# Off-diagonal blocks of the 64x64 inverses: both chunks of a pass at once, even heads from the left and odd heads from the right

## Chip, cores and metric

The kernel runs on one core of one Trainium2 chip. The metric is the device time of one execution in microseconds (us); the number given for the kernel before is the median of three runs. TensorE is called PE here (its weight loads PEld), VectorE DVE, ScalarE ACT, GpSimd POOL and SyncE SP, as in the profile.

## What is computed

Three layers follow each other: a delta-rule linear attention over 4 batches of 8 heads (768 tokens, head size 48), and two feed-forward layers on its 3072 tokens (384 to 2048 to 384).

```python
for t in range(S):                      # attention, per batch and head
    y[t]  = q[t] @ state
    v_old = k_n[t] @ state              # k_n is k divided by its norm
    state = state + beta[t] * outer(k_n[t], v[t] - v_old)
...
h = x @ w_in                            # layer 1
x = where(h > 0, h, exp(min(h, 0)) - 1) @ w_out
h = x @ w_in2                           # layer 2
out = (h * sigmoid(1.702 * h)) @ w_out2
```

All of it is float32. The kernel splits the operands of the feed-forward layers into a high and a low part and does three matmuls for one.

## The kernel before, in words

**Chunks and passes.** The attention is done in 12 chunks of 64 tokens, two to a pass, so there are 6 passes (0 to 5) of 128 tokens. In a chunk the recurrence becomes a triangular system per head, and its 64x64 inverse is needed. The 32 head-batch pairs ("heads" from here) of a chunk lie in 16 columns `u` by two halves of the partitions: partitions 0 to 63 hold one head and 64 to 127 another. A pass holds its inverses in the tile `z`, 128 x 32 x 64; chunk `2p` has `z[:, 0:16]`, chunk `2p + 1` has `z[:, 16:32]`.

**The inverse.** `inverse(p)` (line 199) builds the two 32x32 diagonal blocks of each 64x64 inverse on DVE, both chunks of the pass together; in passes 0 to 2 (`FINE`) it does 16x16 blocks, and `join16` (line 299) joins these by matmuls. The off-diagonal 32x32 block is then formed as minus (inverse of the second block) x (the block of the Gram matrix between them) x (inverse of the first). That takes three steps of `chunk(c)` (line 331), once for each chunk:

- `t2` (line 381): one DVE transpose of the chunk's diagonal blocks, 128 x 512.
- `m1` (line 385): 32 matmuls of 32x32x32 (line 392), each float32 matmul being two records in the trace. Every one reads the partitions 32 to 63 or 96 to 127 and writes 0 to 31 or 64 to 95 of one PSUM bank (`bank()`, tag `at`). ACT evacuates it with two copies of 32 x 512 (line 396) and copies the diagonal blocks beside themselves, 128 x 512 (line 398); POOL clears two pieces of 32 x 512 (line 400).
- `m2` (line 402): 32 matmuls of 32x32x32 (line 407), reading and writing partitions 0 to 31 and 64 to 95, into a bank of the same tag. ACT evacuates with two activations of 32 x 512 (line 412) into `z`.

The other steps of a chunk are `kq` (scores of keys and queries, line 362, masked by DVE in `mask`, line 377), `ks` (keys by state, line 423, subtracted from the values by DVE, line 428), `w` (the inverse times that, line 440, evacuated by ACT), `state` (line 459, added by DVE, line 462), `y` (line 474) and `out` (transposes, line 496). They use the tile `wide()` (line 118): two PSUM banks with one buffer, so that each step that takes `wide` waits until the one before has been evacuated. The tag `at` has one buffer of one bank. PSUM is full: two banks of tag `h`, three of `acc`, two of `wide`, one of `at`.

**The order of the work.** All of it is one list per engine, written in program order (`manual_schedule`). The backbone is 192 units: layer 1 has 96 (6 passes x 16 slices of the 2048 hidden channels), then layer 2. In unit `t`, `up` issues 12 matmuls of 128x128x512 (line 576) and `down` of unit `t - 2` another 12 (line 610; line 621 in layer 2). ACT and DVE turn `h` into `gh` and `gl` between (lines 585 to 601). The attention of pass p is set among the units of layer 1's pass p - 1 by tables in `schedule()` (line 685): a slot `s` means unit `s // 2`, in the middle (`mid`, between `up` and `down`) if even and at its end (`end`, after `down`) if odd. `fill` holds steps of the next inverse and of the weight split, which `spread()` places with the help of `taken`, the load that `VECTOR` (line 943) assigns to a step. Entries of one slot run in the order of the table.

For passes 3 to 5 the table of before (line 851) reads `(6, a, "t2"), (6, a, "m1"), (6, a, "kq"), (8, a, "m2"), (9, b, "t2"), (9, b, "m1"), (9, a, "ks"), (11, b, "m2"), (11, a, "w")`, with `a` and `b` the two chunks. Pass 1 (lines 831 to 835) and pass 2 (line 849) have tables of their own in which these steps lie farther apart. Pass 0 is written out by hand.

Of the kernel before, what the change touches and what calls it, by code (L numbers as in the profile page):

```python
# [9 lines left out]
F32 = mybir.dt.float32  # L10
# [3 lines left out]
AF = mybir.ActivationFunctionType  # L14
# [6 lines left out]
P = 128  # L21
NP = S // P
# [9 lines left out]
class Kernel:  # L32
# [94 lines left out]

    def place(self, c, name):

        if c in (0, 2):  # L130
            x, i = (self.spare[0], 0) if name == "t2" else (self.spare[1], 1024)
            return x[:, i:i + 512].rearrange("p (u t) -> p u t", u=16)
        return self.ap.tile([P, 16, 32], F32, name=name, tag=name)

# [192 lines left out]
        return turned, left, right  # L327

    def chunk(self, c):

# [352 lines left out]
    def schedule(self):  # L685
        nc = self.nc
# [6 lines left out]
        def at(where, u, *fns):  # L693
            where.setdefault(u, []).extend(fns)
# [15 lines left out]

        names = ("nv", "t2", "m1", "kq", "mask", "m2", "ks", "w", "state", "y", "out")
        ch = {c: dict(zip(names, self.later(lambda c=c: list(self.chunk(c).values()), len(names)))) for c in range(NC)}


        spare = self.spare = [self.mp.tile([P, NK * TB], F32, name=n, tag=n) for n in ("xh", "xl")]
# [113 lines left out]
        for slot, c, i in ((5, 2, 0), (5, 2, 1), (7, 2, 2), (8, 3, 0), (8, 3, 1), (10, 3, 2)):  # L829
            at(end if slot % 2 else mid, slot // 2, join[c][i])  # L830
        for slot, c, name in (
# [3 lines left out]
        ):  # L835
            u = slot // 2
            at(end if slot % 2 else mid, u, ch[c][name])
            taken[u] = taken.get(u, 0.0) + self.VECTOR.get(name, 0.0)
        at(end, 7, lambda: self.load_v(3))
# [5 lines left out]
        for p in range(2, NP):  # L845
            o = base[p - 1]
            a, b = 2 * p, 2 * p + 1
            first = (
                (6, a, "t2"), (6, a, "m1"), (8, a, "m2"), (10, a, "kq"), (11, a, "ks"), (12, b, "t2"), (12, b, "m1"), (13, a, "w"), (14, b, "m2"),
            ) if p in self.FINE else (  # L850
                (6, a, "t2"), (6, a, "m1"), (6, a, "kq"), (8, a, "m2"), (9, b, "t2"), (9, b, "m1"), (9, a, "ks"), (11, b, "m2"), (11, a, "w"),
            )
            late = 2 if p in self.FINE else 0
            for slot, c, name in first + (
                (13 + late, a, "state"), (15 + late, a, "y"), (15 + late, b, "nv"), (17 + late, b, "ks"), (19 + late, b, "w"),
                (21 + late, b, "state"), (23, a, "out") if not late else (22, a, "out"), (25, b, "kq"), (27, b, "y"), (29, b, "out"),
            ):
                u = o + slot // 2
                at(end if slot % 2 else mid, u, ch[c][name], *([ch[c]["mask"]] if name == "kq" else []))
                taken[u] = taken.get(u, 0.0) + self.VECTOR.get(name, 0.0)  # L860
            at(end, o - 2, lambda a=a: self.load_kt(a), lambda a=a: self.load_q(a), lambda a=a: self.load_v(a))
            at(end, o - 1, lambda a=a: self.load_kn(a), lambda b=b: self.load_kt(b), lambda b=b: self.load_q(b))
            at(end, o + 2, ch[a]["nv"])
            at(end, o + 5, lambda b=b: self.load_v(b))
            at(end, o + 7, lambda b=b: self.load_kn(b))
            taken[o] = taken.get(o, 0.0) - 0.48
            taken[o + 2] = taken.get(o + 2, 0.0) - 0.48
            taken[o + 1] = taken.get(o + 1, 0.0) + 0.4
        for p in range(2, NP):
            o = base[p - 1]  # L870
# [21 lines left out]
        for t in range(len(units) + self.LAG):  # L892
            if t == len(units):
                low()
            if t < len(units):
                kind, p, c0, n, m = units[t]
# [43 lines left out]
        return [0.1, 1.9, 0.2, 0.7] + [0.8] * (1 if p < 2 else 3) + [1.7, 1.2] + rows + [1.4, 1.9]  # L940


    VECTOR = {"kq": 0.15, "t2": 0.26, "m1": -0.44, "m2": -0.44, "ks": -0.1, "w": -0.44, "state": 0.15, "y": -0.74, "out": 0.17}
    LAG = 2
    N2 = 10
    FINE = 0, 1, 2
# [96 lines left out]
```

## Time and profile before

| what | value |
|---|---|
| device time, median of 3 runs | 1046.31 us (1043.93 to 1048.43) |
| profiled execution, span of the core | 1047.7 us |
| PE busy | 996.2 us, 95% |
| DVE busy | 591.2 us, 56% |
| ACT busy | 453.4 us, 43% |
| POOL busy | 49.5 us, 5% |
| mean granted TensorE clock | 0.974 |

The profile is of one execution, whose span runs from the first to the last instruction; of that execution the page gives the span alone, and it lies within the three runs, 1.4 us above their median. "Granted clock" is the share of full speed that TensorE was given: it has two levels, 1.00 (2.4 GHz) and 0.50 (1.2 GHz). A matmul's row gives when it was issued and how long it took from issue to its last result; since matmuls overlap in the array, the cost of a block of them is read from the start of its first to the start of the next block's first. Idle time stands in brackets with what ended it; "issue" means that the profile shows nothing that was waited for.

### The profile page before, as it was taken

The numbers are of one execution on the slowest core, as the hardware profiler recorded it, in microseconds if no ns is written. First come the engines' busy times: TensorE is split into PE (matmuls) and PEld (weight loads), VectorE is DVE, ScalarE is ACT, GpSimd is POOL, SyncE is SP. The second block draws the span as 40 slices with busy tenths as digits, with TensorE's granted clock in tenths as the row PEclk, the third lists the DMA queues.
The fourth block names the chain that finished last, engine by engine and source line by source line (L and its number), as shares of the span: only waits on it lengthen the run. The fifth ranks groups of instructions, "written<-read, shape, count | busy, mean of one in ns | idle before, by whom it ended". The sixth has DMA issues, their size and how long they took to land.

```text
span 1047.7 us, 26839 instructions
## 1 busy us (share of the span) xinstructions
PE 996.2 (95%) x12136; PEld 854.1 (82%) x12136; DVE 591.2 (56%) x1021; ACT 453.4 (43%) x749; POOL 49.5 (5%) x65
## 2 busy tenths in 40 slices
PE   2678898999999999999999999999999999999998
PEld 2666776877788888888888788999999999999997
DVE  5579568837786777668434676743333333333333
ACT  1254575544445445545544766533333333333322
POOL 2000000000001000000000010000100001000000
PEclk9677999999999999999999999999999999999999
DMA  5252341401220221211001741001010010010000
GB/s 178 114 174 97 114 153 53 132 34 61 63 91 20 72 77 53 71 39 65 18 17 61 281 201 61 1 1 61 1 53 9 1 61 1 23 38 1 31 1 31
DMA packets 20178, 68.40 MB, mean 65 GB/s; under 512 B 3168, under 2 KB 6240, under 8 KB 20064
## 3 DMA queue, kind: packets, MB, share of 16 engines
q1 hardware_dynamic: 20064, 66.69, 18.7%
q8 instruction: 95, 1.56, 0.6%
q14 instruction: 19, 0.16, 0.0%
HBM read 57.25 MB, written 9.44 MB: 64 GB/s over the span
## 4 chain that ended last, share of the span: by engine, by line
PE 92%; DVE 4%; issue 2%; DMA 1%; ACT 1%; SPq 0%; ACTq 0%; DVEq 0%
PE h L576 38%; PE acc L610 18%; PE acc L621 10%; PE accn L621 10%; PE ps_w L362 2%; PE ps_w L474 2%; PE ps_w L459 2%; PE ps_w L188 2%; PE ps_b L392 1%; PE ps_b L407 1%; PE ps_w L423 1%; DMA kg<-in_kT 1%; PE ps_w L440 1%; PE ps_w L496 1%; PE ps_b L323 1%
## 5 line engine op out<-in xcount | busy, mean ns | idle before, releaser
L576 PE MATMUL h<-xh,wt 128*128 128x512 f32 x1152 | 401.0, 402 | 6.4 <-DVE wt L555 5.0
L576 PEld LDWEIGHTS h<-xh,wt 128*128 128x128 f32 x1152 | 219.5, 191 | 53.2 <-DVE wt L555 6.3
L576 PE MATMUL h<-xl,wt 128*128 128x512 f32 x576 | 229.4, 398 | 0.0
L610 PE MATMUL acc<-gh,wt 128*128 128x512 f32 x576 | 197.0, 396 | 0.5 <-DVE xo L674 0.5
L598 ACT CAST gh<-t 128x512 fp32r<-128x512 f32 x192 | 119.2, 621 | 174.8 <-DVE t L589 118.7
L601 DVE TENSOR_TENSOR gl<-t,gh 128x512 fp32r<-128x512 f32 x192 | 138.7, 723 | 68.1 <-PE acc L621 30.9
L595 DVE TENSOR_TENSOR t<-t,h 128x512 f32<-128x512 f32 x96 | 66.0, 688 | 180.3 <-ACT t L592 180.2
L592 ACT ACTIVATE t<-h 128x512 f32<-128x512 f32 x96 | 57.4, 598 | 198.9 <-PE h L576 198.9
L610 PEld LDWEIGHTS acc<-gh,wt 128*128 128x128 f32 x576 | 108.9, 189 | 24.4 <-issue 0.9
L576 PEld LDWEIGHTS h<-xl,wt 128*128 128x128 f32 x576 | 109.8, 191 | 19.2 <-DVE xl L502 0.2
L610 PE MATMUL acc<-gl,wt 128*128 128x512 f32 x288 | 112.9, 392 | 0.0
L589 DVE SCALAR_TENSOR_TENSOR t<-t,h 128x512 f32<-128x512 f32 x96 | 65.6, 684 | 76.2 <-ACT t L586 75.7
L585 ACT ACTIVATE t<-h 128x512 f32<-128x512 f32 x96 | 57.4, 598 | 113.5 <-PE h L576 112.8
L621 PE MATMUL acc<-wt,gh 128*128 128x384 f32 x384 | 98.5, 337 | 0.0
L621 PE MATMUL accn<-wt,gh 128*128 128x384 f32 x384 | 98.1, 336 | 0.0
L621 PEld LDWEIGHTS accn<-wt,gh 128*128 128x128 f32 x384 | 71.0, 188 | 5.4
L621 PEld LDWEIGHTS acc<-wt,gh 128*128 128x128 f32 x384 | 70.3, 188 | 2.8
L621 PE MATMUL acc<-wt,gl 128*128 128x384 f32 x192 | 64.9, 338 | 0.0
L621 PE MATMUL accn<-wt,gl 128*128 128x384 f32 x192 | 64.8, 337 | 0.0
L610 PEld LDWEIGHTS acc<-gl,wt 128*128 128x128 f32 x288 | 54.4, 189 | 10.3
L586 ACT ACTIVATE t<-t 128x512 f32<-128x512 f32 x96 | 60.6, 632 | 3.0
L640 POOL TENSOR_TENSOR xl<-x1r,xh 128x512 fp32r<-128x512 f32 x18 | 24.4, 1355 | 413.9 <-ACT xh L639 321.8
(143 smaller groups left out, 968.7 us busy)
## 6 DMA issues: line engine op xcount, KB each, us to landing
raw<-in_w SPq DMA_DIRECT2D x32, 768.0 KB, 7.4
kt<-in_kT SPq DMA_DIRECT2D x12, 512.0 KB, 4.6
x<-in_qT SPq DMA_DIRECT2D x24, 256.0 KB, 4.2
kg<-in_kT SPq DMA_DIRECT2D x10, 512.0 KB, 4.7
vn<-in_vn SPq DMA_DIRECT2D x12, 384.0 KB, 4.3
kn<-in_kn SPq DMA_DIRECT2D x12, 384.0 KB, 3.6
x1d<-xo SPq DMA_DIRECT2D x12, 384.0 KB, 2.9
x1r<-x1d SPq DMA_DIRECT2D x6, 768.0 KB, 4.6
```

Of the source, the lines that this page charges most:

```text
L188: self.nc.tensor.matmul(o[q:q + 32], k[:, 32 * sub:32 * sub + 32], x, start=True, stop=True)
L576: nc.tensor.matmul(hps, wt[:, part, k * P:(k + 1) * P], src[:, k, c], start=(i == 0), stop=(i == 3 * NK - 1))
L585: nc.scalar.activation(out=t, in_=hps, func=AF.Relu, scale=-1.0)
L586: nc.scalar.activation(out=t, in_=t, func=AF.Exp, scale=-1.0)
L589: nc.vector.scalar_tensor_tensor(out=t, in0=t, scalar=-1.0, in1=hps, op0=ALU.add, op1=ALU.max)
L592: nc.scalar.activation(out=t, in_=hps, func=AF.Sigmoid, scale=1.702)
L595: nc.vector.tensor_tensor(out=t, in0=t, in1=hps, op=ALU.mult)
L598: nc.scalar.copy(gh, t)
L601: nc.vector.tensor_tensor(out=gl, in0=t, in1=gh.bitcast(F32), op=ALU.subtract)
L610: self.nc.tensor.matmul(acc[c], wt[:, part, DM + c * P:DM + (c + 1) * P], src, start=(m == 0 and i == 0), stop=(m == NM - 1 and i == 2),)
L621: self.nc.tensor.matmul(acc[w], src[:, c], wt[:, part, DM:2 * DM], start=(m == 0 and i == 0), stop=(m == NM - 1 and i == 2),)
L640: nc.gpsimd.tensor_tensor(out=xl, in0=raw, in1=xh.bitcast(F32), op=ALU.subtract)
```

## The change

In passes 1 to 5 the steps `t2`, `m1` and `m2` are no longer those of `chunk` but of a new method, `across(p)`, which does each once for both chunks of a pass: one transpose of 128 x 1024, 64 matmuls in `m1` and 64 in `m2`. Heads with even `u` are formed as before, from the left. For heads with odd `u` the product is taken in the other order: `m1` reads the partitions of the first block and writes those of the second, and `m2` reads there and writes the first's. So the matmuls of a step go through four different groups of 32 partitions instead of two. `m1` keeps one bank of tag `at` (the odd heads now fill the other partitions of the same bank) and is evacuated by one copy of 128 x 512; `m2` takes both banks of `wide`, evens in one and odds in the other, and is evacuated by two activations of 32 x 1024. The copy inside `z` is 128 x 1024, the two clears 32 x 1024. The transposed blocks lie in spare tiles in pass 1 and in the tile of tag `kg` in passes 2 to 5. Pass 0 keeps its steps. The tables are rewritten, and three values of `VECTOR`.

```diff
--- before.py
+++ after.py
@@ -127,10 +127,18 @@
 
     def place(self, c, name):
 
-        if c in (0, 2):
+        if c == 0:
             x, i = (self.spare[0], 0) if name == "t2" else (self.spare[1], 1024)
             return x[:, i:i + 512].rearrange("p (u t) -> p u t", u=16)
         return self.ap.tile([P, 16, 32], F32, name=name, tag=name)
+
+    def places(self, p):
+
+        if p == 1:
+            t, m = self.spare[0][:, 0:1024], self.spare[1][:, 1024:1536]
+            return t.rearrange("p (u t) -> p u t", u=32), m.rearrange("p (u t) -> p u t", u=16)
+        t = self.ap.tile([P, 16, 64], F32, name="kg", tag="kg").rearrange("p u (b t) -> p (u b) t", b=2)
+        return t, self.ap.tile([P, 16, 32], F32, name="m1", tag="m1")
 
 
 
@@ -327,6 +335,46 @@
         return turned, left, right
 
 
+
+    def across(self, p):
+
+        nc, pe, act = self.nc, self.nc.tensor, self.nc.scalar
+        s, own = self.pas[p], {}
+
+        def t2():
+            own["t2"], own["m1"] = self.places(p)
+            nc.vector.transpose(out=own["t2"], in_=s["z"][:, :, 0:32])
+
+        def m1():
+            z, t = s["z"], own["t2"]
+            ps = self.bank().rearrange("p (v t) -> p v t", v=16)
+            for u in range(32):
+                for o in (0, 64):
+                    near, far = slice(o, o + 32), slice(o + 32, o + 64)
+                    if u % 2:
+                        pe.matmul(ps[far, u // 2, :], z[near, u, 32:64], t[near, u, :], start=True, stop=True)
+                    else:
+                        pe.matmul(ps[near, u // 2, :], z[far, u, 32:64], z[far, u, 0:32], start=True, stop=True)
+            act.copy(own["m1"], ps)
+            act.copy(z[:, :, 32:64], z[:, :, 0:32])
+            for o in (0, 64):
+                nc.gpsimd.memset(z[o + 32:o + 64, :, 0:32], 0.0)
+
+        def m2():
+            z, t, m = s["z"], own["t2"], own["m1"]
+            ps = self.wide().rearrange("p b (v t) -> p b v t", v=16)
+            for u in range(32):
+                for o in (0, 64):
+                    near, far = slice(o, o + 32), slice(o + 32, o + 64)
+                    a, b = (m[far, u // 2, :], z[far, u, 32:64]) if u % 2 else (t[near, u, :], m[near, u // 2, :])
+                    pe.matmul(ps[near, u % 2, u // 2, :], a, b, start=True, stop=True)
+            for o in (0, 64):
+                near = slice(o, o + 32)
+                act.activation(
+                    out=z[near, :, 32:64].rearrange("p (v b) t -> p b v t", b=2), in_=ps[near], func=AF.Copy, scale=-1.0
+                )
+
+        return dict(t2=t2, m1=m1, m2=m2)
 
     def chunk(self, c):
 
@@ -710,6 +758,10 @@
 
         names = ("nv", "t2", "m1", "kq", "mask", "m2", "ks", "w", "state", "y", "out")
         ch = {c: dict(zip(names, self.later(lambda c=c: list(self.chunk(c).values()), len(names)))) for c in range(NC)}
+        for p in range(1, NP):
+            for name, f in zip(("t2", "m1", "m2"), self.later(lambda p=p: list(self.across(p).values()), 3)):
+                ch[2 * p][name] = f
+                del ch[2 * p + 1][name]
 
 
         spare = self.spare = [self.mp.tile([P, NK * TB], F32, name=n, tag=n) for n in ("xh", "xl")]
@@ -829,8 +881,8 @@
         for slot, c, i in ((5, 2, 0), (5, 2, 1), (7, 2, 2), (8, 3, 0), (8, 3, 1), (10, 3, 2)):
             at(end if slot % 2 else mid, slot // 2, join[c][i])
         for slot, c, name in (
-            (4, 2, "kq"), (4, 2, "mask"), (7, 2, "nv"), (9, 2, "t2"), (9, 2, "m1"), (10, 3, "kq"), (10, 3, "mask"),
-            (11, 2, "m2"), (12, 3, "t2"), (12, 3, "m1"), (13, 2, "ks"), (14, 3, "m2"), (15, 2, "w"), (17, 2, "state"), (17, 3, "nv"),
+            (4, 2, "kq"), (4, 2, "mask"), (7, 2, "nv"), (10, 2, "t2"), (10, 3, "kq"), (10, 3, "mask"),
+            (11, 2, "m1"), (13, 2, "m2"), (13, 2, "ks"), (15, 2, "w"), (17, 2, "state"), (17, 3, "nv"),
             (18, 2, "y"), (20, 3, "ks"), (22, 3, "w"), (24, 3, "state"), (25, 2, "out"), (26, 3, "y"), (28, 3, "out"),
         ):
             u = slot // 2
@@ -846,9 +898,9 @@
             o = base[p - 1]
             a, b = 2 * p, 2 * p + 1
             first = (
-                (6, a, "t2"), (6, a, "m1"), (8, a, "m2"), (10, a, "kq"), (11, a, "ks"), (12, b, "t2"), (12, b, "m1"), (13, a, "w"), (14, b, "m2"),
+                (9, a, "t2"), (10, a, "m1"), (10, a, "kq"), (12, a, "m2"), (12, a, "ks"), (14, a, "w"),
             ) if p in self.FINE else (
-                (6, a, "t2"), (6, a, "m1"), (6, a, "kq"), (8, a, "m2"), (9, b, "t2"), (9, b, "m1"), (9, a, "ks"), (11, b, "m2"), (11, a, "w"),
+                (6, a, "t2"), (6, a, "kq"), (7, a, "m1"), (9, a, "m2"), (9, a, "ks"), (11, a, "w"),
             )
             late = 2 if p in self.FINE else 0
             for slot, c, name in first + (
@@ -940,7 +992,7 @@
         return [0.1, 1.9, 0.2, 0.7] + [0.8] * (1 if p < 2 else 3) + [1.7, 1.2] + rows + [1.4, 1.9]
 
 
-    VECTOR = {"kq": 0.15, "t2": 0.26, "m1": -0.44, "m2": -0.44, "ks": -0.1, "w": -0.44, "state": 0.15, "y": -0.74, "out": 0.17}
+    VECTOR = {"kq": 0.15, "t2": 0.55, "m1": -0.5, "m2": -0.5, "ks": -0.1, "w": -0.44, "state": 0.15, "y": -0.74, "out": 0.17}
     LAG = 2
     N2 = 10
     FINE = 0, 1, 2
```

## Rows read from the trace of the kernel before

**Rows 1.** The page: span, TensorE's busy time, and the chain by engine.
```profile
span 1047.7 us, 26839 instructions
...
PE 996.2 (95%) x12136; PEld 854.1 (82%) x12136; DVE 591.2 (56%) x1021; ACT 453.4 (43%) x749; POOL 49.5 (5%) x65
...
PE 92%; DVE 4%; issue 2%; DMA 1%; ACT 1%; SPq 0%; ACTq 0%; DVEq 0%
```

**Rows 2.** Windows: busy us (count) of PE, PEld, DVE, ACT, POOL; granted clock; DMA.
```profile
160.00:200.00 40.00, 36.80 (x629) 29.49 (x628) 34.23 (x75) 21.46 (x34) 1.20 (x2) 0.96 0.35 111
320.00:360.00 40.00, 40.00 (x720) 32.88 (x719) 29.03 (x65) 18.00 (x30) 3.34 (x5) 1.00 0.19 58
230.00:1047.00 817.00, 812.54 (x7466) 702.28 (x7464) 436.94 (x734) 348.06 (x570) 35.47 (x35) 1.00 0.15 50
```

**Rows 3.** Timeline of PE, pass 5: start us, us, line, tiles, count.
```profile
506.14 0.39 PE L576 MATMUL h<-xl,wt 128*128 128x512 f32 x1
506.36 0.39 PE L576 MATMUL h<-xh,wt 128*128 128x512 f32 x1
506.68 1.20 PE L407 MATMUL ps_b<-m,t 32*32 32x32 f32 x64
507.81 0.50 PE L610 MATMUL acc<-gh,wt 128*128 128x512 f32 x1
508.15 0.40 PE L610 MATMUL acc<-gl,wt 128*128 128x512 f32 x1
...
511.21 1.15 PE L423 MATMUL ps_w<-su,kt 48*64 48x48 f32 x64
512.28 0.50 PE L576 MATMUL h<-xh,wt 128*128 128x512 f32 x1
```

**Rows 4.** Timeline of PE, pass 2: a block of `join16`, then a gap inside one.
```profile
209.98 1.26 PE L315 MATMUL ps_b<-kg,z 32*32 32x16 f32 x128
211.17 0.50 PE L610 MATMUL acc<-gh,wt 128*128 128x512 f32 x1
...
215.34 0.85 PE L323 MATMUL ps_b<-w 16*32 16x16 f32 x79 [1.31 <-issue]
```

**Rows 5.** Timeline of PE, pass 1: two more gaps.
```profile
126.38 0.45 PE L362 MATMUL ps_w<-x,kt 48*64 48x64 f32 x8 [0.86 <-issue]
...
135.83 1.15 PE L423 MATMUL ps_w<-su,kt 48*64 48x48 f32 x64
138.05 1.48 PE L188 MATMUL ps_w<-kg 48*32 48x64 f32 x128 [1.08 <-DVE r L428]
```

**Rows 6.** Groups of instructions from 114 to 600 us: busy us, mean ns.
```profile
L412 ACT ACTIVATE z<-ps_b 32x512 f32<-32x512 f32 x20 | 11.7, 583 | 0.7 <-PE ps_b L407 0.5
...
L428 DVE TENSOR_TENSOR r<-vn,ps_w 128x768 f32<-128x768 f32 x10 | 9.5, 954 | 15.2 <-PE ps_w L423 15.2
...
L194 ACT COPY z<-ps_w 128x1024 f32<-128x1024 f32 x7 | 7.1, 1013 | 4.9 <-PE ps_w L188 4.9
L383 DVE STREAM_TRANSPOSE t<-z 128x512 f32<-128x512 f32 x9 | 6.3, 705 | 0.0
```

**Rows 7.** Windows behind gaps of TensorE; granted clock behind POOL's column.
```profile
126.40:178.00 51.60, 48.25 (x911) 38.44 (x911) 40.54 (x65) 32.69 (x53) 2.62 (x4) 1.00 0.31 106
...
178.90:182.20 3.30, 3.27 (x11) 2.92 (x12) 1.14 (x3) 1.58 (x3) 0.00 (x0) 0.50 0.00 0
...
216.50:219.80 3.30, 3.30 (x9) 2.31 (x7) 2.85 (x5) 0.00 (x0) 0.00 (x0) 0.50 0.02 7
```

**Rows 8.** Chain of waits in order of time: start us, us, what.
```profile
216.18 3.84 PE h L576 x9
...
224.61 2.26 PE h L576 x9
```

**Rows 9.** Waits of PE: us in total, times, longest us.
```profile
PE ps_w L496 <- DVE su L462: 2.6, 1, 2.6
...
PE ps_w L423 <- DVE x L377: 0.4, 1, 0.4
```

## The prediction

> **What bounds the kernel now.** I read the page first. TensorE is busy for 996.2 of 1047.7 us, and 92% of the chain that ended last is its own work [rows 1]. Since a busy share is an average, I then went through windows of 40 us. In those of passes 3 to 5 PE is busy from end to end at the full granted clock, while DVE has some 29 of 40 us and ACT 18; one of pass 3 stands for them [rows 2]. So in these passes a microsecond counts only if it is one of PE's: ACT and DVE work taken away is worth nothing by itself, and whatever PE must wait for is added whole. PE works through its list in order, and layer 2 follows on the same engine, so nothing later absorbs a shift. In passes 1 and 2 there are a few waits of PE; the largest is 2.6 us for the sum of the states [rows 9].
>
> **What the small blocks cost.** The reader should look at starts, not durations. An `m2` block of one chunk starts at 506.68 and the next block at 507.81: 1.13 us for 64 records. Before it the start-to-start step is 0.32 us where large matmuls keep 0.22 (506.14 to 506.36), and behind it 0.34 (507.81 to 508.15): changing over from large matmuls and back costs 0.2 us on top [rows 3]. `m1` has the same shape and takes the same 1.13 us. The changed blocks have 128 records over four groups of partitions. The nearest row is a block of `join16`, whose 32x32 stationary tiles also go through four groups: 128 records in 1.19 us (209.98 to 211.17) [rows 4]. Its moving side is 16 wide, not 32, so I take 1.25 us for each new block. The ends are 1.19 us and 2.26 us (twice 1.13, nothing side by side).
>
> **What PE saves, pass by pass.** In passes 3 to 5 the four blocks stand as `m1` with `kq`, `m2` alone, `m1` with `ks`, `m2` with `w`: 4 x 1.13 + 0.2 = 4.72 us. Afterwards `m1` is alone and `m2` stands before `ks`: 2 x 1.25 + 0.2 = 2.70. Saved: 2.02 a pass, 6.1 in three. In pass 1 all four were alone, 4 x 1.33 = 5.32, against 2.70: 2.6. In pass 2 they were alone too, and afterwards both have company (`kq`, `ks`): 5.32 - 2.50 = 2.8. There `ks` also waited 0.4 us for the mask to leave `wide` [rows 9]; now it comes a whole unit after `kq` instead of half a unit, so that goes: 3.2. Together 11.9 us.
>
> **What PE gains in waiting.** This is the step that decides. `m2` now takes `wide`, the next entry of its slot in all five passes is `ks`, and `ks` takes `wide` too. There is one buffer, so `ks`, and with it everything behind it on PE, stands until ACT has evacuated `m2`. Before, `m2` was in the other tag and a whole `down` or `up` lay behind it. The evacuation is two activations of 32 x 1024. The trace has 32 x 512 at 0.58 us and a 128 x 1024 copy out of the same tile at 1.01 [rows 6], and two of a pair run one after the other (20 of them are 11.7 us of busy time): 2.02 us. The handover I take from pass 1, where a Gram block waits for `ks` to be taken out of `wide`: 135.83 to 138.05 is 2.22 us [rows 5], the block alone 1.07 (511.21 to 512.28) [rows 3], DVE's subtraction 0.95 [rows 6], which leaves 0.2. So 2.2 us a pass, 11.0 in all. It could be 1.2 more a pass if ACT still had two instructions of 512 before it (2 x 0.58); less is excluded by the order. Behind the waiting `ks` on PE is all of the unit; DVE's subtraction for `r` waits as well, and behind it on DVE the steps of the next inverse and `gl` of the unit. `gl` is needed two units later, some 8 us, so PE does not wait a second time.
>
> **What the clock takes.** I compare four gaps of PE with the granted clock behind them. Idle times of 0.86 us and 1.08 us [rows 5] left it at 1.00 from 126.4 to 178 us [rows 7]. Idle 1.31 us [rows 4], and the 2.6 us of the wait for the states [rows 9], were each followed by a window at 0.50, which is 1.2 GHz [rows 7]. The new gap of about 2.1 us idle lies among those that fell, and small blocks stand on both sides of it, as at 215.34. A fall costs 1.6 us: one `up` took 3.84 us instead of 2.26 [rows 8]. The fall follows at some distance from the gap (216.5 after 215.34), not with it, so a gap can be missed: I take four of five, 6.4 us. The ends are none and 8.0.
>
> **What the denser blocks may cost.** Inside dense blocks PE sometimes stands with nothing named: 1.31 us in the second `join16` block that followed another by one `down` [rows 4], 0.86 us in a `kq` right behind such a block [rows 5]. Pass 1 now has `m1` one `down` behind `join16` and `kq`, and pass 2 has `kq` right behind `m1`: I put 2.0 us there, between 0 and 7 (1.4 in each of the five passes).
>
> **What costs nothing.** DVE: two transposes of 0.705 us [rows 6] become one of 1.4 to 2.0; it hides in DVE's 11 idle us of 40 [rows 2], and without that cover the mask, and `m2` behind it on `wide`, would come up to 0.6 us late. ACT loses six instructions a pass, POOL has half as many twice as long; both are done within the unit before `w`, and if not, `w` waits up to 1 us. In pass 2 `state` comes half a unit after `w` instead of a whole one: `down` covers ACT's two copies between them, and if it does not, `state` waits for one ACT instruction of 512, 0.6 us. No DMA is moved and SP's order stays; `kg` is taken when no load into it is due for some units.
>
> **Sum.** -11.9 + 11.0 + 6.4 + 2.0 = +7.5 us: the profiled 1047.7 becomes 1055.2. That span is 1.4 us above the median, so the forecast is 1046.3 + 7.5 = 1053.8 us.
>
> **Rivals.** *The clock holds.* If gaps of this length pass unpunished and the dense blocks run through, the sum is -11.9 + 11.0 = -0.9: 1045.4 us; with the 2.0 us it is 1047.4. For it speaks that the clock stays at 1.00 from 230 us to the end [rows 2]; against it that PE has no gap there that could be held beside the new one.
>
> *The groups do not run side by side.* The change would then not do what it says. All of `m1` writes one bank from four groups; if that ran in turn, each `m1` keeps 2.26 us, +5.0 in five passes, 1058.8; with `m2` as well 1063.8. Against it: the `join16` block does exactly this, four groups into one bank, at 1.19 us for 128 records [rows 4]. The Trainium skill states on this, in TensorEngine Tiling, section Gotcha 1: PSUM Pressure, that different row tiles cannot use one PSUM bank at the same time. By that rule `m1` would gain nothing and the time would be 1058.8; the row of `join16` disagrees with this reading of it, since its four groups write different partitions, as those of `m1` do.
>
> *Faster: the wait for the states goes.* At 176 us `out` waits 2.6 us for DVE's sum of the states [rows 9], and a fall of the clock follows, 1.6 us [rows 7]. If PE's new stand in pass 1 lets DVE get 2.6 us ahead by then, both go: with the clock held elsewhere -0.9 - 4.2 = -5.1, and with blocks at 1.19 us another -0.6, so 1040.6. It decides only if DVE's lag is older than pass 1's `m2`. I see the opposite: DVE is busy for 34.2 of the 40 us from 160 on [rows 2], long after that block, so the lag is made there.
>
> **Numbers.** Forecast 0.55, clock holds 0.22, no overlap 0.13, faster 0.10. A measurement of this kernel can tell about 0.5%, 5.2 us, from no change. Of the forecast, which is +7.5 with four falls and +4.3 with two, 0.46 is slower and 0.09 the same; the held clock gives 0.21 the same and 0.01 faster; no overlap 0.12 slower and 0.01 the same. Faster 0.11, same 0.31, slower 0.58. The range runs from 1043 (part of the faster rival) to 1060 (m1 without overlap, or more gaps of the dense blocks).
>
> **What would show it.** `m1` and `m2` of 128 records at 1.2 to 1.3 us from start to start; in each of five passes a wait of `ks` on PE for ACT's evacuation, 2.1 us idle, led by two activations of 1.0 us; the granted clock at 0.50 behind most of them, and a mean below 0.974. I am wrong if that wait is missing or much shorter, if the clock stays at 1.00 behind it, or if the blocks take over 2 us.

## The result, and the profile after

The changed kernel takes 1058.94 us (median of 4 runs, 1052.92 to 1061.86) against 1046.57 for the kernel before: a ratio of 1.0109, 95% interval 1.0072 to 1.0146. Twelve more runs beside the kernel before on another chip gave 1.0076 (1.0049 to 1.0104). It is slower by about 1%. The forecast, 1053.8 us or 1.0072 of the median it started from, has the direction and lies 5.1 us below the time; the range holds it.

The page of the changed kernel, in the lines that answer to [rows 1]:

```profile
span 1055.0 us, 26776 instructions
...
PE 991.4 (94%) x12136; PEld 849.3 (80%) x12136; DVE 587.8 (56%) x1016; ACT 442.2 (42%) x719; POOL 48.6 (5%) x55
...
PE 90%; DVE 4%; ACT 2%; issue 2%; DMA 1%; SPq 0%; ACTq 0%; DVEq 0%
```

PE is busy for 4.8 us less than before, and the span is 7.3 us longer. So PE has less to do and stands longer. Where it stands, the list of PE's waits says (us in total, times, longest). Lines have moved: L373 is the evacuation behind `m2`, L471 is `ks`, L370 `m2`'s matmuls, L355 and L357 those of `m1`, L624 `up`, L658 `down`.

```profile
PE ps_w L471 <- ACT z L373: 10.7, 5, 2.1
...
PE ps_w L544 <- DVE su L510: 2.7, 1, 2.7
```

The first row is new: five waits of `ks` for ACT, 2.14 us each and 10.7 in all, one in each pass from 1 to 5. The second answers to the wait for the states in [rows 9] and is about as long as it was. In pass 5 the timeline of PE shows the new blocks and the wait (start us, us):

```profile
510.24 0.39 PE L658 MATMUL acc<-gh,wt 128*128 128x512 f32 x1
510.56 0.22 PE L357 MATMUL ps_b<-z 32*32 32x32 f32 x2
...
511.77 0.50 PE L624 MATMUL h<-xh,wt 128*128 128x512 f32 x1
```

```profile
515.76 0.39 PE L658 MATMUL acc<-gh,wt 128*128 128x512 f32 x1
516.08 0.22 PE L370 MATMUL ps_w<-m,kg 32*32 32x32 f32 x2
...
519.51 1.15 PE L471 MATMUL ps_w<-su,kt 48*64 48x48 f32 x64 [2.14 <-ACT z L373]
520.58 0.50 PE L624 MATMUL h<-xh,wt 128*128 128x512 f32 x1
```

Reading starts: `m1` runs from 510.56 to 511.77, 1.21 us for 128 records, where [rows 3] has 1.13 for a block of 64. `m2` starts at 516.08, `ks` at 519.51: 3.42 us, of which 2.33 lie between the issue of the last matmul of `m2` and `ks`. Where no wait follows, 0.12 us lie there, and `m2` takes 1.22 us from start to start, as much as `m1`; the first experiment shows such a block. So the wait adds 2.2 us. What PE waited for is on ACT, two activations in 2.04 us:

```profile
517.41 2.04 ACT L373 ACTIVATE z<-ps_w 32x1024 f32<-32x1024 f32 x2 [0.63 <-PE ps_w L370]
```

Behind the five waits the granted clock (the column after POOL's) was at half, 0.50, in passes 1, 2 and 3 and full, 1.00, in passes 4 and 5:

```profile
139.40:146.10 6.70, 6.37 (x138) 5.11 (x139) 2.79 (x4) 1.90 (x3) 0.00 (x0) 0.50 0.16 48
245.20:251.90 6.70, 6.69 (x75) 5.60 (x76) 4.11 (x12) 0.62 (x1) 0.00 (x0) 0.50 0.20 61
337.30:340.70 3.40, 3.40 (x9) 2.65 (x9) 3.09 (x11) 0.00 (x0) 0.00 (x0) 0.50 0.39 120
428.00:445.00 17.00, 14.86 (x241) 12.21 (x240) 8.55 (x20) 7.30 (x11) 0.07 (x1) 1.00 0.15 46
517.00:535.00 18.00, 15.86 (x286) 13.00 (x273) 6.13 (x8) 8.02 (x12) 0.00 (x0) 1.00 0.14 46
```

One more row belongs to pass 2, a gap inside `kq`, which now stands right behind `m1`:

```profile
235.59 0.63 PE L410 MATMUL ps_w<-x,kt 48*64 48x64 f32 x15 [1.17 <-issue]
```

Two further entries of PE's list bear on the account. `up` waits 1.5 us for `gl` from DVE at 118.90 us, ahead of the new steps of pass 1. The profile of the kernel before has no such wait, five of the nine profiles of the other kernels have it, and no run shows what brings it:

```profile
118.90 0.73 PE L624 MATMUL h<-xh,wt 128*128 128x512 f32 x2 [1.50 <-DVE gl L649]
```

And the wait for the states was followed by half clock in the kernel before [rows 7], but not here: from 178 to 200 us the clock is 1.00.

**Where the time went, pass by pass.** The table gives how much later (+) or earlier each kernel's backbone got in a stretch, against the kernel before: the difference of the starts of `up` at the end of a stretch, less that at its beginning, both from the traces. The stretch of pass 1 runs from the start of `up` in unit 4 to that in unit 8; those of passes 2 to 5 run from unit 18 to 24, 34 to 41, 49 to 57 and 65 to 73. Between passes 2 and 3, 3 and 4, 4 and 5, and behind pass 5 nothing moved by more than 0.1 us; the stretch from unit 8 to 18, left out of the table, moved by -1.2 to +0.5 us (+5.9 in the kernel with `out` moved, +1.7 in the last).

| kernel | to unit 4 | pass 1 | pass 2 | pass 3 | pass 4 | pass 5 | at the end |
|---|---|---|---|---|---|---|---|
| changed, first profile | -0.1 | +3.2 | +3.1 | +1.7 | +0.1 | +0.2 | +7.3 |
| changed, second profile | -0.4 | +3.5 | -0.7 | +3.3 | +3.2 | +3.1 | +12.0 |
| `m2` and `ks` apart | -3.4 | +0.5 | -4.8 | -1.3 | -1.9 | -0.5 | -11.4 |
| wait filled with work | -2.7 | +2.7 | -2.7 | -0.3 | +0.1 | +0.2 | -2.9 |
| two groups at a time | 0.0 | +2.8 | +3.2 | +4.8 | +3.3 | +3.4 | +16.4 |
| longer evacuation | -3.9 | +3.3 | +3.2 | +4.9 | +2.7 | +3.7 | +12.7 |
| apart, Gram block moved | -1.9 | +3.3 | -2.6 | -1.6 | -1.9 | -0.3 | -4.5 |
| the same, `out` moved | +0.6 | -6.2 | -5.4 | -1.7 | -1.9 | +1.0 | -7.8 |
| Gram block moved, list shifted | +3.4 | -0.8 | -4.4 | -2.3 | -1.9 | -1.8 | -5.9 |

The start differs by up to 4 us from one execution to the next. Pass 1 stands in the part where PE's clock goes up and down anyway, and in pass 2 the kernel before has a gap and a fall of its own ([rows 4], [rows 7]); passes 3 to 5 show the change most clearly. Passes 4 and 5 of the first profile, at full clock, come out at +0.1 and +0.2 us: what the blocks save and what `ks` waits cancel there.

### The profile page after: what moved, and what is told of

Same layout as the page of the kernel before. It is cut to its first block, busy times and chain, and to the rows that moved or that the text cites. A ratio compares the mean times of both kernels' runs of the same rounds, so it can differ in the third digit from the quotient of the medians.

```text
span 1055.0 us, 26776 instructions
## 1 busy us (share of the span) xinstructions
PE 991.4 (94%) x12136; PEld 849.3 (80%) x12136; DVE 587.8 (56%) x1016; ACT 442.2 (42%) x719; POOL 48.6 (5%) x55
## 4 chain that ended last, share of the span: by engine, by line
PE 90%; DVE 4%; ACT 2%; issue 2%; DMA 1%; SPq 0%; ACTq 0%; DVEq 0%
PE h L624 38%; PE acc L658 18%; PE acc L669 10%; PE accn L669 10%; PE ps_w L410 2%; PE ps_w L522 2%; PE ps_w L507 2%; PE ps_w L196 1%; PE ps_w L471 1%; ACT z L373 1%; PE ps_w L488 1%; PE ps_b L331 1%; DMA raw<-in_w 1%; DVE wt L603 1%; DMA kg<-in_kT 1%
## 5 line engine op out<-in xcount | busy, mean ns | idle before, releaser
L624 PE MATMUL h<-xh,wt 128*128 128x512 f32 x1152 | 402.0, 403 | 7.7 <-DVE wt L603 4.9
L624 PEld LDWEIGHTS h<-xh,wt 128*128 128x128 f32 x1152 | 219.6, 191 | 55.6 <-DVE wt L603 6.2
L624 PE MATMUL h<-xl,wt 128*128 128x512 f32 x576 | 229.8, 399 | 0.0
L658 PE MATMUL acc<-gh,wt 128*128 128x512 f32 x576 | 196.6, 396 | 0.6 <-DVE xo L722 0.6
L658 PEld LDWEIGHTS acc<-gh,wt 128*128 128x128 f32 x576 | 109.2, 190 | 24.8 <-issue 0.9
L624 PEld LDWEIGHTS h<-xl,wt 128*128 128x128 f32 x576 | 110.1, 191 | 19.5 <-DVE xl L550 0.2
L658 PE MATMUL acc<-gl,wt 128*128 128x512 f32 x288 | 113.0, 392 | 0.0
L658 PEld LDWEIGHTS acc<-gl,wt 128*128 128x128 f32 x288 | 54.5, 189 | 10.9
```

Source lines behind the costliest of these rows:

```text
L624: nc.tensor.matmul(hps, wt[:, part, k * P:(k + 1) * P], src[:, k, c], start=(i == 0), stop=(i == 3 * NK - 1))
L658: self.nc.tensor.matmul(acc[c], wt[:, part, DM + c * P:DM + (c + 1) * P], src, start=(m == 0 and i == 0), stop=(m == NM - 1 and i == 2),)
```

## The experiments

Two theories stood against each other: that the loss is the wait of `ks` for `wide` and the fall of the clock behind it, or that the dense blocks themselves, or the clock without the wait, take back what they save. Times of one batch are compared with the kernel before on the same chip.

**`m2` and `ks` apart.** Nothing but places in the tables changes:

```diff
-            (11, 2, "m1"), (13, 2, "m2"), (13, 2, "ks"), (15, 2, "w"), (17, 2, "state"), (17, 3, "nv"),
+            (11, 2, "m1"), (12, 2, "m2"), (13, 2, "ks"), (15, 2, "w"), (17, 2, "state"), (17, 3, "nv"),
...
-                (9, a, "t2"), (10, a, "m1"), (10, a, "kq"), (12, a, "m2"), (12, a, "ks"), (14, a, "w"),
+                (9, a, "t2"), (10, a, "m1"), (10, a, "kq"), (12, a, "m2"), (13, a, "ks"), (14, a, "w"),
...
-                (6, a, "t2"), (6, a, "kq"), (7, a, "m1"), (9, a, "m2"), (9, a, "ks"), (11, a, "w"),
+                (6, a, "t2"), (6, a, "kq"), (7, a, "m1"), (8, a, "ks"), (9, a, "m2"), (11, a, "w"),
```

> The changed kernel with m2 and ks set half a unit apart (ks a half unit earlier in passes 3 to 5, m2 or ks moved in passes 1 and 2), so that a whole down or up lies between the two users of wide. Theory (the wait of ks for the evacuation of m2, 2.33 us from start to start in each of five passes, and the clock falls behind it make the loss): the five waits go, the granted clock stays at 1.00 from 110 us on but for the falls that the kernel before has too, and the time is 1046.6 less 13 us of saved blocks plus 1 us of new change-overs plus 1 to 2 us of unnamed gaps: about 1036 us, 10 us under the kernel before. Rival (the dense blocks themselves starve PE and pull the clock down, the wait is a symptom): the gaps move elsewhere, the clock still falls in passes 1 to 3, and the time stays above 1046 us.

Measured: 1043.21 us (12 runs, 1038.25 to 1052.70) against 1048.71, a ratio of 0.9955 (0.9927 to 0.9983). Against the two ratios of the changed kernel that is 1.2 and 1.5% less from a reordering alone. The blocks are the same; `m2` of pass 4 on its own takes 1.22 us (412.12 to 413.34), and in passes 2 to 5 the clock stays at 1.00 (window from 181 to 600 us):

```profile
412.12 0.22 PE L370 MATMUL ps_w<-m,kg 32*32 32x32 f32 x2
...
413.34 0.50 PE L624 MATMUL h<-xh,wt 128*128 128x512 f32 x1
```

```profile
181.00:600.00 419.00, 414.82 (x6275) 339.53 (x6272) 278.89 (x535) 200.98 (x321) 13.97 (x13) 1.00 0.24 81
```

So the wait, and not the blocks, carried the loss. What lies between the two users of `wide` is one `up` or `down`, nine matmuls of 128x128x512 each in layer 1, not the twelve given above ([rows 8] has `x9`). The forecast of 10 us under the kernel before was too good by half, by the times. Passes 1 and 5 show a part of why: pass 5 gains only 0.5 us, with a gap of 1.1 us inside `m2` that has no named cause, and pass 1 gains nothing. The profiled execution is the fastest of the twelve, so the rest is not in this trace. Pass 1's waits of PE (us, times, longest), and a window right behind them:

```profile
PE ps_w L196 <- DVE r L476: 1.1, 1, 1.1
...
PE ps_w L471 <- ACT z L373: 0.9, 1, 0.9
```

```profile
136.00:139.30 3.30, 3.30 (x43) 2.65 (x43) 0.92 (x2) 1.90 (x3) 0.00 (x0) 0.50 0.02 5
```

Half a unit was not enough there, because ACT, which has a piece of the weights to convert (L599) first, starts on `m2` only at 129.65:

```profile
128.93 0.82 ACT L599 CAST wt<-w 128x768 fp32r<-128x768 f32 x1
129.65 2.04 ACT L373 ACTIVATE z<-ps_w 32x1024 f32<-32x1024 f32 x2
```

So `ks` still waits 0.9 us, the Gram block waits for `ks` as it did in [rows 5], and the clock falls (0.50).

**The wait filled.** `ks` still has to wait for `wide`, but PE does something:

```diff
                     pe.matmul(ps[near, u % 2, u // 2, :], a, b, start=True, stop=True)
+            busy = self.bank()
+            for i in range(8):
+                pe.matmul(busy, self.wt[0, 0][:, 0, 0:P], self.x["a", p - 1][0][:, 0, :], start=True, stop=True)
```

> The changed kernel with eight 128x128x512 matmuls whose result nobody reads, set between m2 and ks into the bank of m1, 8 x 0.227 = 1.8 us, so that PE works while it would wait. The wait for wide itself stays. Theory (part of the loss is the clock that falls behind the idle 2.1 us): no window at 0.50 behind the five places, the step from pass to pass falls to that of passes 4 and 5 of the changed kernel (about +0.2 us against before, +0.2 for the change-over), passes 1 and 2 keep their unnamed gaps; time about 1048 us, some 10 us under the changed kernel. Rival (the clock falls for the small blocks, not for the idle time, or the falls cost nothing): the windows at 0.50 stay or go without effect, and the time stays at 1056 us or above.

Measured: 1049.85 us (12 runs) against 1048.71, 1.0022 (0.9999 to 1.0045): 0.5 to 0.9% under the two ratios of the changed kernel. The windows around the five places (granted clock behind POOL's column):

```profile
136.00:142.60 6.60, 5.92 (x136) 4.78 (x137) 3.35 (x5) 1.90 (x3) 0.00 (x0) 0.50 0.10 19
238.00:250.00 12.00, 11.89 (x228) 9.40 (x217) 5.52 (x15) 6.25 (x9) 0.00 (x0) 1.00 0.14 37
330.00:345.00 15.00, 15.00 (x202) 12.09 (x201) 9.72 (x26) 6.42 (x10) 0.00 (x0) 1.00 0.27 90
420.00:445.00 25.00, 24.90 (x396) 20.41 (x396) 16.95 (x40) 9.71 (x16) 0.00 (x0) 1.00 0.25 75
510.00:535.00 25.00, 25.00 (x378) 20.46 (x371) 10.31 (x14) 9.79 (x15) 0.00 (x0) 1.00 0.12 34
```

Behind the places in passes 2 to 5 the clock stays at 1.00, and the table has these passes at -2.7, -0.3, +0.1 and +0.2 us: in passes 3 to 5 the saving and the filled wait nearly cancel, with nothing lost to the clock, and in pass 2 the fall that the kernel before has there is gone as well. In pass 1 it falls even so (0.50 from 136 us), behind the Gram block's wait for `ks`, which this kernel keeps. So the wait costs twice: once itself (0.7%, this kernel against the one with `ks` apart), and once by the clock (the 0.5 to 0.9%).

**Two groups at a time.** All even heads first, then all odd ones, in `m1` and `m2`:

```diff
-            for u in range(32):
+            for u in [*range(0, 32, 2), *range(1, 32, 2)]:
```

> The changed kernel with the matmuls of m1 and m2 in another order: all even heads first, then all odd ones, so that neighbours go through two groups of partitions and not four. Theory (the saving is that four groups run side by side): m1 and m2 of 128 records take 2.26 us each from start to start instead of 1.21 and 1.09, 2.2 us a pass, 11 us in all: about 1069 us, or 2 to 3 less where the longer blocks keep the clock up. Rival (the blocks are short because there are fewer of them and fewer change-overs): the blocks stay near 1.2 us and the time is that of the changed kernel.

Measured: 1065.90 us (4 runs) against 1048.71, 1.0163 (1.0134 to 1.0192). The timeline of PE in pass 5 has `m2` in its two halves, by the names of the operands (start us, us, count):

```profile
522.56 0.39 PE L658 MATMUL acc<-gh,wt 128*128 128x512 f32 x1
522.88 1.10 PE L370 MATMUL ps_w<-m,kg 32*32 32x32 f32 x58
...
523.89 1.11 PE L370 MATMUL ps_w<-z,m 32*32 32x32 f32 x59
527.14 1.33 PE L471 MATMUL ps_w<-su,kt 48*64 48x48 f32 x64 [2.14 <-ACT z L373]
528.40 0.79 PE L624 MATMUL h<-xh,wt 128*128 128x512 f32 x1
```

From 522.88 to 527.14 are 4.26 us, 0.84 more than the 3.42 of the changed kernel, with the same wait behind. So `m2` takes 2.06 us instead of 1.22, and `m1` in this profile 2.05 (516.52 to 518.57), with the same number of matmuls and change-overs and the same banks. It is the alternation over four groups that saves, 0.84 us a block. The size was forecast as 1.1; 128 records of two groups in one block take a little less than twice 1.13.

**A longer evacuation.** The second activation is done twice:

```diff
-            for o in (0, 64):
+            for o in (0, 64, 64):
                 near = slice(o, o + 32)
```

> The changed kernel with the second activation behind m2 done twice (same values), so that the evacuation of wide is three times 1.01 us instead of two. Theory (ks, and all of PE behind it, waits for the whole evacuation): the wait from start to start grows from 2.33 to 3.34 us in all five passes, 5 us, and the clock falls behind each of them, another 2 to 4 us: 1064 to 1068 us. Rival (PE would have waited for something else anyway): the time moves by less than 2 us.

Measured: 1065.41 us (4 runs) against 1048.71, 1.0163 (1.0118 to 1.0207). The waits of PE, and the evacuation's row (duration ns min/median/max):

```profile
PE ps_w L471 <- ACT z L373: 15.9, 5, 3.2
```

```profile
L373 ACT ACTIVATE z<-ps_w x15: 1012/1015/1015, 130.3 to 521.5; 32x1024 f32<-32x1024 f32 x15
```

Five more activations of 1.015 us, 5.1 us, and PE's five waits grow from 10.7 to 15.9: PE waits for the whole of it, one for one.

**The changed kernel again.**

> The changed kernel once more, unaltered, beside the next two on one chip, because its four runs lay between 1052.9 and 1061.9 us. Theory: the five waits of 2.33 us from start to start are there in every run, and the number of windows at 0.50 behind them (three places of five in the first profile) differs from run to run: 1.0 to 1.3% over the kernel before, with runs some 8 us apart. Rival (the loss of the first four runs was their chip's): within 0.7% of the kernel before.

Measured: 1059.05 us (12 runs, 1051.77 to 1068.14) against 1049.90, 1.0076 (1.0049 to 1.0104). That is less than the 1.0 to 1.3% of the theory and just above the rival's 0.7%: the loss is not the first chip's alone, but the two ratios do not settle its size more closely than 0.8 to 1.1%. The five waits are there again. In this profile the clock fell behind all of them; the windows:

```profile
139.00:145.50 6.50, 5.30 (x135) 4.32 (x136) 3.17 (x5) 1.90 (x3) 0.00 (x0) 0.50 0.02 5
244.70:247.90 3.20, 3.20 (x38) 2.62 (x32) 2.24 (x6) 0.62 (x1) 0.00 (x0) 0.50 0.16 20
333.40:340.10 6.70, 6.70 (x75) 5.55 (x76) 4.24 (x14) 0.60 (x1) 0.00 (x0) 0.50 0.19 61
429.00:435.70 6.70, 6.70 (x75) 5.59 (x76) 4.25 (x14) 0.57 (x1) 0.00 (x0) 0.50 0.18 59
521.20:527.90 6.70, 6.55 (x75) 5.49 (x76) 1.55 (x2) 0.51 (x2) 0.00 (x0) 0.50 0.18 61
```

Passes 4 and 5 cost +3.2 and +3.1 us here and +0.1 and +0.2 in the first profile, with the same waits: 3.0 us is what a fall of 6.7 us costs. The one of 3.4 us behind pass 3 of the first profile cost 1.5 (+1.7 less 0.2). The number and length of the falls can thus set executions several us apart. The twelve runs lie up to 16 us apart; the fastest has a mean clock of 0.985 and the slowest 0.965, but the clock does not order all twelve, so a part of the spread stays open.

**The Gram block moved.** In pass 1 `ks` stands half a unit ahead of `m2`, and the second Gram block of pass 2 stands in the middle of unit 8; passes 2 to 5 are as in the first experiment:

```diff
-            (11, 2, "m1"), (13, 2, "m2"), (13, 2, "ks"), (15, 2, "w"), (17, 2, "state"), (17, 3, "nv"),
+            (11, 2, "m1"), (12, 2, "ks"), (13, 2, "m2"), (15, 2, "w"), (17, 2, "state"), (17, 3, "nv"),
...
-                self.passes(at, spread, end, fill, p, (3, 6), (9, o + 2), lambda: turned(2))
+                self.passes(at, spread, end, fill, p, (3, 8), (9, o + 2), lambda: turned(2), mid)
...
-        at(end, grams[1], lambda: self.gram(2 * p + 1, self.kg))
+        at(end if second is None else second, grams[1], lambda: self.gram(2 * p + 1, self.kg))
```

> The kernel with m2 and ks apart, and pass 1 mended as well: ks at the middle and m2 at the end of unit 6, the second Gram block of pass 2 moved from the end of unit 6 to the middle of unit 8, so that every two users of wide have a half unit between them there too. In the kernel with m2 and ks apart pass 1 still had 0.86 us of ks behind the evacuation of m2, 1.06 us of the Gram block behind ks, and a window at 0.50. Theory (each of these waits is a second user of wide coming too early): 0.9 + 1.1 + 1.6 us less, about 3.5 us under that kernel: 10 to 14 us under the kernel before by the traces from the third unit on, 1.0% by the times. Rival (pass 1 is bound by the unnamed gaps): the waits go but PE stands elsewhere in pass 1 and the time stays within 1 us of that kernel, 0.5% under before.

Measured: 1043.03 us (12 runs, 1035.81 to 1048.77) against 1049.90, 0.9929 (0.9900 to 0.9957). It beats both kernels: 6.9 us under the one before, 16 under the changed one on the same chip. Against the first experiment it gains 0.26%, 2.7 us, which the two intervals do not separate. Three rows of the waits of PE in its profile:

```profile
PE ps_b L331 <- issue: 5.5, 3, 2.7
...
PE ps_w L370 <- issue: 3.4, 2, 2.1
PE ps_w L544 <- DVE su L510: 2.7, 1, 2.7
```

Neither `ks` behind ACT nor the Gram block behind DVE is left. In their place stand waits for nothing that the profile names, inside `join16` and `m2`; with them pass 1 of this execution came out at +3.3 us. Both theories had a part: the 0.7% lie between the 1.0% of the one and the 0.5% of the other.

**`out` moved as well.**

```diff
-            (18, 2, "y"), (20, 3, "ks"), (22, 3, "w"), (24, 3, "state"), (25, 2, "out"), (26, 3, "y"), (28, 3, "out"),
+            (18, 2, "y"), (20, 3, "ks"), (22, 3, "w"), (24, 3, "state"), (26, 2, "out"), (27, 3, "y"), (29, 3, "out"),
```

> The same, and out of chunk 2 moved from the end of unit 12 to the middle of unit 13, with y and out of chunk 3 half a unit later each. In all kernels so far out waits 2.6 us there for the sum of the states on DVE, and in most profiles a window at 0.50 follows. Theory: both go, 2.6 + 1.6 = 4.2 us under the kernel with the Gram block moved. Rival (DVE is late by itself there, and PE meets the lag at the next step that needs it): the wait moves to y or to the next up, and less than 1.5 us is gained.

Measured: 1046.97 us (12 runs) against 1049.90, 0.9972 (0.9944 to 1.0000): no gain over the kernel with the Gram block moved. This theory fell. The timelines of PE and of DVE there (start us, us, idle before):

```profile
175.89 0.85 PE L544 MATMUL ps_w<-ident,y 128*128 128x128 f32 x6 [0.61 <-DVE su L510]
...
182.13 2.73 PE L522 MATMUL ps_w<-su,x 128*64 128x48 f32 x64 [3.34 <-DVE xl L550]
```

```profile
173.83 1.92 DVE L510 TENSOR_TENSOR su<-su,ps_w 48x768 f32<-48x768 f32 x2
...
177.73 0.95 DVE L603 TENSOR_TENSOR wt<-w,wt 128x768 fp32r<-128x768 f32 x1
...
181.43 0.56 DVE L550 TENSOR_TENSOR xl<-ps_w,xh 128x384 fp32r<-128x384 f32 x1 [0.55 <-ACT xh L549]
```

The states' sum starts at 173.83 and `out` waits only 0.61 us for it, but `y` (L522) now waits 3.34 us for DVE to take `out`'s result from `wide` (L550, 181.43), because DVE has its list in between, the weights' split (L603) among it. Behind the new wait the clock is 0.50 from 183.4 to 190 us, while behind the 2.7 us of `out` in the kernel with the Gram block moved it stayed at 1.00. DVE is late in this stretch, and PE meets that at the next step, as the rival had it.

**The instruction list shifted.** In the kernel with the Gram block moved, half of `m1` of pass 1 issued twice:

```diff
-            for u in range(32):
+            for u in [*range(16), *range(32)] if p == 1 else range(32):
```

> The kernel with the Gram block moved, and the first 32 matmuls of m1 in pass 1 issued twice (same values): 64 more records at 10 ns, 0.6 us, which shift the place of every later instruction in PE's list by half of the 127 records that lie between the unnamed gaps. So far these gaps sat at the same places of the list in every kernel (records 4300, 6085 and 9143, counted from the start), each 1.3 to 1.5 us behind the end of a 16 KB transfer of the instruction queue. Theory (PE runs out of instructions where a stretch between two such places is dense): the places stay where they are in the count, so the blocks meet them elsewhere: the gap of 1.3 to 2.6 us inside m2 of pass 5 and the one inside the second join16 block of pass 2 (1.5 us) go or fall under 0.5 us; others may come. Rival (something in those blocks makes PE wait, such as a bank or the blocks' own data): both gaps stay in m2 and join16, now 64 records later in the count.

Measured, with one run of each: 1043.89 us, and 1048.70 for the kernel before. The gap that the kernel without the shift has inside `m2` of pass 5, on its timeline of PE,

```profile
508.65 0.22 PE L370 MATMUL ps_w<-z,m 32*32 32x32 f32 x2 [1.34 <-issue]
```

is gone: that block takes 1.22 us from start to start, and pass 5 comes out at -1.8 us instead of -0.3. In `join16` of pass 2 the gap fell from 1.5 us from start to start to 0.69, and new ones came into `m2` of pass 2 and, of 1.9 us, into the doubled `m1` of pass 1 (two stretches of the shifted kernel's timeline of PE):

```profile
217.78 1.13 PE L331 MATMUL ps_b<-w 16*32 16x16 f32 x113
219.42 0.31 PE L331 MATMUL ps_b<-w 16*32 16x16 f32 x15 [0.52 <-issue]
```

```profile
242.53 0.21 PE L370 MATMUL ps_w<-m,kg 32*32 32x32 f32 x2 [0.88 <-issue]
```

Counting all matmul records from the start, the gaps inside blocks of the two kernels lie at 2261, 2644, 2900, 3027, 4300, 4428, 4811, 5067, 6085 and 9143: always a multiple of some 127.4 records from the first. The shift moved the blocks over these places and not the places with the blocks. A place shows as a gap only where a dense stretch lies over it: of the nine profiles without the shift eight have one at 4300, six at 6085 and three at 9143, so the expectation, which has them in every kernel, goes too far. One gap without a named cause is of another kind: 0.75 us ahead of `state` at 275.66 us lies between two blocks, is no multiple away (5507) and moved with its block by 64 records.

## Why the prediction was right, point by point

- **What bounds.** PE's list, from end to end: passes 3 to 5 moved the backbone by what happened on PE, and nothing was taken back behind them (+7.2 us at unit 73, +7.3 at the end).
- **The blocks.** Taken at 1.25 us each, measured 1.21 and 1.22. By the same working the saving is 2.1 us in each of passes 3 to 5, 2.7 in pass 1 and 3.3 in pass 2, 12.2 in all instead of 11.9. The rival that the groups do not run side by side is out: with two groups at a time the blocks take 2.05. `m1`, with four groups in one bank, and `m2`, with its even and odd heads in two banks, take the same. The Trainium skill states (TensorEngine Tiling (Array Packing), section Gotcha 1: PSUM Pressure) that different row tiles cannot use one bank at the same time. That did not show in `m1`, whose groups write different partitions; two groups on the same partitions of one bank were not tried.
- **The wait.** Taken at 2.2 us in five places, and 2.2 in five is what it added: 11.0 in all, as forecast. The longer evacuation showed that it follows ACT one for one, the version with `ks` apart that it goes when the two users of `wide` are apart. Saving and wait of passes 4 and 5 give -2.1 + 2.2 = +0.1, and the table has +0.1 and +0.2.
- **The clock.** This term was right in kind and wrong in size. It was four falls of 1.6 us, 6.4. The profiles have falls in three passes of five and in all five, some of 3.4 us at a cost of 1.5 and most of 6.7 us at a cost of 3.0. The rows of before had only falls of the short kind behind a single gap, and I took their price for all. What is left of the two spans when saving and wait are taken out, 7.3 + 1.2 = 8.5 us in the first profile and 12.0 + 1.2 = 13.2 in the second, is clock, unnamed gaps and the differing starts together; the forecast had 8.4.
- **The dense blocks.** 2.0 us of unnamed gaps: one of 1.17 us idle came in pass 2 inside `kq` behind `m1`, as expected; in pass 1 the first profile has one of 1.1 us in `join16`, where the kernel before had others. The term can't be read off singly.
- **What costs nothing** cost nothing in the first profile as far as the new steps go: no other wait of theirs stands in PE's list. The 1.5 us that `up` waits for `gl` ahead of them were not foreseen, and whether the change brings them is open.
- **The rivals.** The filled wait comes nearest to the held clock: it gives 1.0022, by that ratio 2.3 us over the kernel before, where -0.9 us was worked out, or +1.1 with the gaps of the dense blocks; in pass 1 its clock still fell. That the wait for the states would go did not happen (2.7 us again). With `out` moved PE met DVE's lag one step later, which fits the reason given, that the lag is made in that stretch.
- **The sum.** The two spans differ by +7.3 us, the sum was +7.5, and that they meet is in part luck: the second profile has +12.0. A run takes 1.7 us longer than its span (1056.71 us for 1055.0), so by this estimate the execution behind [rows 1] took 1049.4 us and lay 3.1 us over the median; the 1.4 us given ahead set a span beside times. The changed one lay 2.2 us under its median. The medians are 12.4 us apart.

## What to carry to other kernels

When a step moves to another PSUM tile, look at who takes that tile next and how soon: here the move was needed for the faster blocks, and the next entry of the same slot took the tile too, so that PE stood for the evacuation; half a unit between the two users turned +0.8 to +1.1% into -0.45%, and into -0.7% with the Gram block moved too. A short stand of TensorE can cost twice, once itself and once by the clock behind it; here, filling it with matmuls that nobody needs saved the second in four passes of five. In these blocks of 32x32x32, going round four groups of partitions in turn instead of two took 1.22 us instead of 2.06 for 128 records.

## What was not expected of the hardware

PE stops inside dense stretches of small matmuls for 0.3 to 2.7 us with nothing named, at places of its instruction list some 127.4 matmul records apart, and each of these gaps ended 1.2 to 1.6 us after a 16 KB transfer of the instruction queue. The page of the kernel with the Gram block moved has that queue (transfers, MB, share of the engines):

```profile
q8 instruction: 95, 1.56, 0.6%
```

Between the gaps at 217.30 and 508.65 us in that kernel lie 38 steps of 127.4 records, and 38 of these transfers end. That the places belong to the list and not to the blocks is shown by the shifted kernel, in one profile; that PE has run out of instructions there is argued from the transfers, and no run changed them. A transfer takes about 1.0 us (0.9 to 1.7), and 1.2 to 1.6 more pass before PE goes on, while a stretch of 128 records takes 1.1 us. A version that places its dense blocks by these steps was not tried.
